# Moving GpSimd's division, the gather and the feed-forward layers by half a step in an attention kernel with routed rows

## The chip, the cores and the metric

The kernel runs on one core of one Trainium2 chip. A core has a matrix engine (TensorE, "PE" in the profile, with its weight loads as "PEld"), a vector engine (VectorE, "DVE"), an engine for activation functions and copies (ScalarE, "ACT"), a general engine (GpSimd, "POOL") and SyncE ("SP"), which here only issues DMAs. Each engine takes its own instructions in the order in which they were issued and waits on semaphores for the others. The metric is the time of one execution on the device in microseconds, the median of several runs.

## The reference

Two blocks in sequence: an attention with queries averaged in pairs, and a layer that passes only the 128 best-scored rows of each batch through a small network.

```python
B, H, S, D = 8, 8, 1152, 64            # attention; then rows of H * D = 512, F = 1024
q_pool = q.reshape(B, H, S // 2, 2, D).mean(axis=3)
attn = softmax(q_pool @ k.T / sqrt(D))
x = (attn @ v) -> (B, S // 2, H * D)   # heads side by side
scores = einsum('bsd,d->bs', x, w_gate)
out = x.copy()
for b in range(B):
    top_idx = argpartition(-scores[b], 128)[:128]
    xe = x[b, top_idx]
    ye = maximum(xe @ w1, 0) @ w2
    out[b, top_idx] = xe + sigmoid(scores[b, top_idx])[:, None] * ye
```

## The kernel before

All is float32. Two heads make a pair, four pairs a batch, 32 pairs in all. A pair's 576 averaged queries are split into two halves of 288, so that the main loop in `run` goes over 64 halves; half h has s = h % 2, and "even" and "odd" below mean s = 0 and s = 1. Each half is worked on over several turns of the loop (a turn is also called a half below, by the half whose scores it computes):

- turn h: `scores` (L818): 9 chunks of 4 matmuls with 64 rows each, keys down the partitions. ScalarE takes the exponential of each chunk (L825) into `p`. `folded` sums over the keys: GpSimd adds two thirds of the chunks (three instructions, L857, into `acc`), VectorE folds the last third and then `acc` (L862, two instructions) and reduces both to `sum` (L872).
- turn h + 1: `weighted` (L836): 36 matmuls that multiply `p` with the values. ScalarE copies the result out of PSUM (`two`, L844), GpSimd adds its two parts (`av`, L846), and `drained` transposes that on VectorE (`avb`, L915).
- turn h + 2: `multiplied`: GpSimd multiplies `avb` with the gate's weights (`prod`, L925).
- turn h + 3: `gated`: VectorE sums that (`red`, L979) and, with the pair's second half, divides it by the sums of exponentials (`part`, L981).

The sums of a pair come from 4 groups of partitions: ScalarE puts them side by side (`groups`, L887, in an even turn), VectorE adds them (`total`, L893), and ScalarE spreads the total over the partitions (`sums`, L902, in the odd turn). `normalized`, at the end of an odd turn, takes the reciprocal (`rec`, L954, VectorE) and multiplies `avb` by it on GpSimd (`x`, L956). `stored` sends `x` to the output (L968) two turns later. Even turns also prepare the next pair: GpSimd adds the queries (`qp`, L732), VectorE transposes keys and queries (`kT`, `qT`, L735 and L739). SyncE's queue has the loads of keys, queries and values, the stores and some small transfers of the routing, in the order of issue.

When a batch's last pair is gated, in turn h0 = 8b + 10, the generator `routed` begins for it. It does the row routing in pieces and stops at each `yield`. The mark that it yields says where it goes on: in `units(mid=True)`, called after the scores and before the weighted values of a turn, or in `units(mid=False)`, at the turn's end. Its pieces: sums of the gate's scores and their copy through DRAM (h0 + 1), counting ranks on VectorE (L1083, L1092, L1102; ends of h0 + 3, h0 + 4, h0 + 5), ranks and gates through DRAM to all partitions (`lines`, end of h0 + 5), two searches for slot i's row and gate (`pick`, L1166, end of h0 + 6), the row's number as an integer (`index`, L1175, GpSimd), the gather of the 128 rows from the output (L1183, an indirect DMA from GpSimd's queue), their transposes (L1197, TensorE, middle of h0 + 8), layer one (L1208, 32 matmuls, middle of h0 + 9), layer two (L1221, 8 matmuls, middle of h0 + 10), the scaling (`y`, L1240, ScalarE), the addition (L1245, GpSimd) and the scatter (L1246, an indirect DMA). A batch begins every 8 turns, so that the layers of one batch fall beside the first pieces of the next.

Batch 5 stops after layer one and batch 6 before its layers; both go on at the end, when the last batch is ranked: their matmuls fill TensorE's waits for it. The last batch's row of scores is made on TensorE (L1054) from `diag` (L1044), and its sums by a matmul (L938). `pieces(unit, n)` runs n pieces of a unit. The names at the end: `older`, `old` and `new` are batches 5, 6 and 7.

Of the kernel before, what the change touches and what calls it, by code (L numbers as in the profile page):

```python
# [10 lines left out]
P = 128  # L11
BLK = 32
# [522 lines left out]
class _Plain:  # L535
# [396 lines left out]
    def normalized(self, pair):  # L932

        nc, hp = self.nc, pair["hp"]
        tot = self.sums[:, pair["b"] * self.NPAIR + hp, :]
        if self.last_pair(pair):
            ps = self.banks()[:, 0, :]
            nc.tensor.matmul(  # L938
                ps[:, 0 : 2 * self.QB],
                lhsT=self.merge.rearrange("p g j -> p (g j)"),  # L940
                rhs=pair["sum"].rearrange("p j n -> p (j n)"),
                start=True,
                stop=True,
            )
            for j in range(2):
                rows = slice(j * self.D, (j + 1) * self.D)
                nc.scalar.activation(
                    tot[rows, :],
                    ps[rows, j * self.QB : (j + 1) * self.QB],
                    AF.Identity,  # L950
                    bias=self.tiny[rows, 0:1],
                )
        rec = pair["rec"] = self.small.tile([P, self.QB], F32, name="rec")
        nc.vector.reciprocal(rec[:, :], tot)  # L954
        x = self.work.tile([P, self.QB, BLK], F32, name="x")
        nc.gpsimd.tensor_tensor(  # L956
            out=x[:, :, :],
            in0=pair["avb"][:, :, :],
            in1=rec[:, :].unsqueeze(2).broadcast_to([P, self.QB, BLK]),
            op=ALU.mult,  # L960
        )
        pair["x"] = x

    def stored(self, pair):

# [7 lines left out]
    def gated(self, half):  # L973

        nc, pair, hb = self.nc, half["pair"], self.HB
        if half["s"] == 0:
            pair["red"] = self.small.tile([P, self.QB], F32, name="red")
        ns = slice(half["s"] * hb, (half["s"] + 1) * hb)
        nc.vector.tensor_reduce(pair["red"][:, ns], pair["prod"][:, ns, :], AX.X, ALU.add)  # L979
        if half["s"] == 1:  # L980
            nc.vector.tensor_tensor(  # L981
                out=pair["part"][:, pair["hp"], :],
                in0=pair["red"][:, :],
                in1=pair["rec"][:, :],
                op=ALU.mult,
            )
            if pair["hp"] == self.NPAIR - 1:
                unit = self.routed(pair["b"], pair["part"])
                at = next(unit) == "mid"
                self.routing.append([pair["b"], unit, at])  # L990

# [3 lines left out]
    def routed(self, b, part):  # L997
# [139 lines left out]
        for s0, w in self.slots:  # L1137
# [3 lines left out]
            if b == self.B - 1:  # L1141

                nc.vector.tensor_tensor(
                    out=pick[:, :, 0:w],
                    in0=self.slot_f[:, s0 : s0 + w].unsqueeze(1).broadcast_to([P, NT, w]),
                    in1=rank[:, :].unsqueeze(2).broadcast_to([P, NT, w]),
                    op=ALU.is_equal,
                )
                yield True
                ps = self.banks()[:, 0, 0:2]  # L1150
                for t, rows in tiles:
                    nc.tensor.matmul(
                        ps[0:w, :],
                        lhsT=pick[0:rows, t, 0:w],
                        rhs=meta[0:rows, t, :],
                        start=(t == 0),
                        stop=(t == NT - 1),
                    )
                nc.scalar.copy(index[0:w, :], ps[0:w, 0:1])
                nc.scalar.copy(own_gate[0:w, :], ps[0:w, 1:2])  # L1160
            else:
                yield True

                found = self.small.tile([P, 1], F32, name="found_token")
                for of, to in ((self.token_line, found), (lines[:, :, 1, :], own_gate)):
                    nc.vector.scalar_tensor_tensor(  # L1166
                        out=pick.rearrange("p t i -> p (t i)").rearrange("p (i t) -> p i t", t=NT)[0:w],
                        in0=lines[0:w, :, 0, :],
                        scalar=self.token[0:w, s0 // P : s0 // P + 1],
                        in1=of[0:w, :, :],  # L1170
                        op0=ALU.is_equal,
                        op1=ALU.mult,
                        accum_out=to[0:w, :],
                    )
                nc.gpsimd.tensor_scalar(  # L1175
                    out=index[0:w, :],
                    in0=found[0:w, :],
                    scalar1=float(b * Sp),
                    scalar2=None,
                    op0=ALU.add,  # L1180
                )
            xe = ffn.tile([P, self.Dm], F32, name="xe")
            nc.gpsimd.indirect_dma_start(  # L1183
                out=xe[0:w, :],
# [4 lines left out]
                oob_is_err=False,  # L1189
            )  # L1190
            yield True
            yield mid

            xeT = ffn.tile([P, self.ND, P], F32, name="xeT")
            pv = self.banks()[:, 0, :].rearrange("p (c n) -> p c n", n=P)
# [94 lines left out]
        )  # L1290
        return count_i

    def units(self, mid):


        for entry in self.routing[::-1]:
            b, unit, at = entry
            if b in self.waiting or at != mid:
                continue
            end = next((mark for mark in unit if mark), None)  # L1300
            if end is None:
                self.routing.remove(entry)
            elif end == "hidden" and b == self.B - 3:
                self.waiting.add(b)
            entry[2] = end in ("mid", "hidden") and b < self.B - 2

    def run(self):
        nc = self.nc
# [10 lines left out]
            self.load_values(loaded)  # L1319
        self.load_gate()  # L1320
        weights = self.weight_loads()
        for h in range(n_halves + 1):
            if h < n_halves:
                n, s = divmod(h, 2)
                if s == 0:
                    pair = upcoming
                    if pair["hp"] == 0:
                        part = self.ffn.tile([P, self.NPAIR, self.QB], F32, name="part")
                    pair["part"] = part
                else:  # L1330
                    loaded = None
                    if n + 2 < len(pairs):
                        loaded = self.load_pair(*pairs[n + 2])
                        self.load_values(loaded)
                    if n > 1:
                        self.stored(halves[h - 4]["pair"])
                if h > 1:
                    next(weights, None)
                half = {"pair": pair, "s": s}
                halves.append(half)  # L1340
                self.scores(half)
                if h > 1:

                    of = halves[h - 2 - s]["pair"]
                    if s == 0:
                        of["groups"] = self.side_by_side(of["sum"].rearrange("p j n -> p (j n)"))
                    else:
                        self.spread(of)
                self.units(mid=True)
                if h > 2:  # L1350
                    self.gated(halves[h - 3])
                self.folded(half)
                if h > 1:
                    self.multiplied(halves[h - 2])
                if s == 0 and loaded:
                    upcoming = loaded
                    self.prepare_pair(upcoming)
            else:
                self.stored(halves[h - 3]["pair"])
                self.gated(halves[h - 3])  # L1360
                self.multiplied(halves[h - 2])
                self.units(mid=True)
                self.units(mid=False)
            if h > 0:
                done = halves[h - 1]
                self.weighted(done)
                self.drained(done)
            if h == n_halves:
                self.multiplied(done)
                self.gated(halves[h - 2])  # L1370
            if 1 < h < n_halves and s == 0:
                done["pair"]["total"] = self.added(done["pair"]["groups"])
            if h == n_halves:
                self.normalized(done["pair"])
            elif h > 2 and s == 1:
                self.normalized(halves[h - 2]["pair"])
            if h < n_halves:
                self.units(mid=False)
        for _ in weights:
            pass  # L1380

        self.stored(halves[-1]["pair"])


        self.gated(halves[-1])
        left = [unit for _, unit, _ in self.routing]
        new = left.pop()
        old = left.pop() if left else iter(())
        older = left.pop() if left else iter(())
        assert not left  # L1390

        def pieces(unit, n=None):
            for i, _ in enumerate(unit):
                if i + 1 == n:
                    break

        pieces(older, self.NFC - 2)
        pieces(new, 1)
        pieces(older, 2)
        pieces(new, 3)  # L1400
# [71 lines left out]
```

## Time and profile before

| what | us |
|---|---|
| median of 3 runs (708.6 to 709.43) | 708.87 |
| the profiled execution | 706.64 |
| its span, first to last instruction | 704.8 |
| TensorE busy, 9948 matmul records | 694.4 |
| VectorE busy | 496.5 |
| GpSimd busy | 485.1 |
| ScalarE busy | 444.5 |

A line of a timeline gives the start in us from the beginning of the span, the duration, the engine, the line of the code, the operation, what it writes and reads, and how many instructions were merged (x72: each float32 matmul has two records). Square brackets hold the idle time of the engine before it and what ended it. Matmul ends are modelled, so that neighbouring groups overlap by some tenths: distances are taken from start to start. Among the groups of the page, with busy time, mean duration and idle time before them:

```profile
L857 POOL TENSOR_TENSOR acc<-p 128x576 f32<-128x576 f32 x192 | 266.3, 1417 | 15.4 <-ACT p L825 15.1
L846 POOL TENSOR_TENSOR av<-two 128x288 f32<-128x288 f32 x64 | 51.2, 800 | 96.5 <-ACT two L844 94.9
L956 POOL TENSOR_TENSOR x<-avb,rec 128x576 f32<-128x576 f32 x32 | 37.1, 1159 | 40.3 <-DVE rec L954 27.9
L732 POOL TENSOR_TENSOR qp<-qb 128x576 f32<-128x576 f32 x31 | 43.8, 1414 | 2.2 <-DMA qb<-in_q_dram 2.2
```

### The profile page before, as it was taken

How to read it: one execution, taken by the hardware profiler on the slowest of the kernel's cores; microseconds unless marked ns; L12 is line 12 of the kernel's file. 1: busy time of each engine (PE TensorE's matmuls, PEld its weight loads, DVE VectorE, ACT ScalarE, POOL GpSimd, SP SyncE). 2: the span in 40 equal slices, each digit the busy share in tenths (PEclk: the TensorE clock that was granted, in tenths of full speed). 3: DMA queues.
4: the chain of work that ended last, by engine and by line, in shares of the span. 5: the costliest groups of instructions: out<-in, count | busy, mean ns of one | idle time of the engine just before them, and what ended most of it. 6: DMA issues, size and time to landing. Idle time of an engine off the chain costs nothing.

```text
span 704.8 us, 23397 instructions
## 1 busy us (share of the span) xinstructions
PE 694.4 (99%) x9948; PEld 516.8 (73%) x9948; DVE 496.5 (70%) x793; ACT 444.5 (63%) x963; POOL 485.1 (69%) x452
## 2 busy tenths in 40 slices
PE   8999999999999999999999999999999999999996
PEld 5668899996758866688656887578775787766573
DVE  3877777996559965498754988559774697689540
ACT  6677778777547775477746776467754777477210
POOL 5877777868658695586955779467874877686520
PEclk9999999999999999999999999999999999999999
DMA  8888887858486483756928468382775728432200
GB/s 175 172 178 180 171 166 137 146 116 161 85 149 111 85 162 75 145 97 111 172 40 159 81 129 160 66 148 61 161 130 85 135 56 169 83 72 62 45 31 35
DMA packets 389490, 82.86 MB, mean 118 GB/s; under 512 B 376640, under 2 KB 376640, under 8 KB 389376
## 3 DMA queue, kind: packets, MB, share of 16 engines
q1 hardware_dynamic: 387872, 76.49, 58.1%
q0 software_dynamic: 1280, 4.20, 1.8%
q8 instruction: 80, 1.31, 0.8%
q10 hardware_dynamic: 224, 0.59, 0.3%
q14 instruction: 34, 0.28, 0.1%
HBM read 69.65 MB, written 11.59 MB: 115 GB/s over the span
## 4 chain that ended last, share of the span: by engine, by line
PE 89%; POOL 5%; issue 2%; DMA 1%; ACT 1%; DVE 1%; SPq 0%; POOLq 0%; DVEq 0%; ACTq 0%
PE ps L836 36%; PE ps L818 36%; PE ps L1208 8%; PE ps L1221 7%; POOL acc L857 2%; ACT p L825 1%; DMA kb<-in_k_dram 1%; DMA xe<-out_dram,index 1%; PE ps L1197 1%; POOL prod L925 1%; POOL x L956 0%; POOL av L846 0%; DVE fold L862 0%; POOL index L1175 0%; SPq L759 0%
## 5 line engine op out<-in xcount | busy, mean ns | idle before, releaser
L825 ACT ACTIVATE p<-ps 128x576 f32<-128x576 f32 x576 | 320.2, 695 | 1.7 <-PE ps L818 1.3
L818 PE MATMUL ps<-qT,kT 64*64 64x288 f32 x4608 | 295.2, 404 | 0.2 <-ACT p L825 0.2
L836 PE MATMUL ps<-p,v_sb 64*64 64x288 f32 x4608 | 294.6, 403 | 0.0
L857 POOL TENSOR_TENSOR acc<-p 128x576 f32<-128x576 f32 x192 | 266.3, 1417 | 15.4 <-ACT p L825 15.1
L836 PEld LDWEIGHTS ps<-p,v_sb 64*64 64x64 f32 x4608 | 215.5, 133 | 65.3 <-ACT p L825 9.2
L818 PEld LDWEIGHTS ps<-qT,kT 64*64 64x64 f32 x4608 | 208.0, 132 | 73.0 <-ACT p L825 15.4
L862 DVE TRANSPOSE_TENSOR_REDUCE fold<-p 128x54 f32<-128x1728 f32 x64 | 126.0, 1969 | 50.2 <-ACT p L825 50.2
L862 DVE TRANSPOSE_TENSOR_REDUCE fold<-acc 128x54 f32<-128x1728 f32 x64 | 125.3, 1957 | 46.0 <-POOL acc L857 45.8
L844 ACT COPY two<-ps 128x576 f32<-128x576 f32 x64 | 40.9, 639 | 156.9 <-PE ps L836 143.8
L846 POOL TENSOR_TENSOR av<-two 128x288 f32<-128x288 f32 x64 | 51.2, 800 | 96.5 <-ACT two L844 94.9
L915 DVE STREAM_TRANSPOSE avb<-av 128x288 f32<-128x288 f32 x64 | 29.4, 460 | 66.5 <-POOL av L846 66.5
L956 POOL TENSOR_TENSOR x<-avb,rec 128x576 f32<-128x576 f32 x32 | 37.1, 1159 | 40.3 <-DVE rec L954 27.9
L1208 PEld LDWEIGHTS ps<-xeT,w 128*128 128x128 f32 x512 | 57.8, 192 | 2.7 <-ACT p L825 2.6
L1208 PE MATMUL ps<-xeT,w 128*128 128x128 f32 x512 | 59.3, 277 | 0.0
L1221 PE MATMUL ps<-w,hT 128*128 128x512 f32 x128 | 57.3, 598 | 0.0
L925 POOL TENSOR_TENSOR prod<-avb,w_gate 128x288 f32<-128x288 f32 x64 | 51.5, 805 | 0.6 <-DVE avb L915 0.6
L902 ACT ACTIVATE sums<-total,tiny 32x18 f32<-32x18 f32 x124 | 38.1, 308 | 15.9 <-DVE total L893 14.2
L732 POOL TENSOR_TENSOR qp<-qb 128x576 f32<-128x576 f32 x31 | 43.8, 1414 | 2.2 <-DMA qb<-in_q_dram 2.2
L1221 PEld LDWEIGHTS ps<-w,hT 128*128 128x128 f32 x128 | 23.6, 190 | 28.1 <-issue 25.8
L735 DVE STREAM_TRANSPOSE kT<-kb 128x1152 f32<-128x1152 f32 x31 | 42.5, 1370 | 0.0
L887 ACT COPY groups<-sum 32x36 f32<-32x36 f32 x124 | 27.1, 219 | 6.7 <-DVE sum L872 5.2
L981 DVE TENSOR_TENSOR part<-red,rec 128x18 f32<-128x18 f32 x32 | 27.0, 845 | 1.1
(95 smaller groups left out, 290.6 us busy)
## 6 DMA issues: line engine op xcount, KB each, us to landing
kb<-in_k_dram SPq DMA_DIRECT2D x124, 144.0 KB
qb<-in_q_dram SPq DMA_DIRECT2D x124, 144.0 KB
v_sb<-in_v_dram SPq DMA_DIRECT2D x124, 144.0 KB
out_dram<-x SPq DMA_DIRECT2D x128, 72.0 KB
lines<-row_rank SPq DMA_DIRECT2D x7, 640.0 KB
w<-in_moe_w_dram SPq DMA_DIRECT2D x8, 512.0 KB
sc_row<-row SPq DMA_DIRECT2D x7, 288.0 KB
acc<-in_q_dram ACTq DMA_DIRECT2D x2, 288.0 KB
```

Source lines behind the costliest of these rows:

```text
L732: nc.gpsimd.tensor_tensor(out=qp[:, :, :], in0=pair["q"][:, :, 0, :], in1=pair["q"][:, :, 1, :], op=ALU.add)
L735: nc.vector.transpose(kT.rearrange("p (c g i) -> p c g i", c=self.NC, i=BLK), pair["k"].rearrange("p (g c) d -> p c g d", c=self.NC),)
L818: nc.tensor.matmul(sc[keys, j, 0:n], lhsT=pair["kT"][rows, c * P + keys.start : c * P + keys.stop], rhs=pair["qT"][rows, qs], start=True, ...
L825: nc.scalar.activation(p[:, c // G, c % G, :, :], sc[:, :, 0:n], AF.Exp, scale=self.scale)
L836: nc.tensor.matmul(av[j * self.D : (j + 1) * self.D, e, 0:n], lhsT=half["pair"]["v"][keys, j, c, :], rhs=half["p"][keys, c // G, c % G, j, :],
L844: nc.scalar.copy(two[:, :, :], av[:, :, 0:n])
L846: nc.gpsimd.tensor_tensor(out=half["av"][:, :], in0=two[:, 0, :], in1=two[:, 1, :], op=ALU.add)
L857: nc.gpsimd.tensor_tensor(out=acc[:, u, :], in0=units[:, 0, u, :], in1=units[:, 1, u, :], op=ALU.add)
L862: nc.vector.tensor_reduce(fold[:, a, :], of.rearrange("p u (m d) -> p (u m) d", d=BLK), AX.X, ALU.add, apply_transpose=True,)
L925: self.nc.gpsimd.tensor_tensor(out=pair["prod"][:, ns, :], in0=pair["avb"][:, ns, :], in1=self.w_gate[:, hp : hp + 1, :].broadcast_to([P, ...
L1208: nc.tensor.matmul(pv[:, f, 0:w], lhsT=self.w1[:, c, (f0 + f) * P : (f0 + f + 1) * P], rhs=xeT[:, c, 0:w], start=(c == 0), stop=(c == self ...
L1221: nc.tensor.matmul(ps[0:w, 0 : self.Dm], lhsT=hT[:, f, 0:w], rhs=self.w2[:, f, :], start=(f == 0), stop=(f == self.NFC - 1),)
```

## The change

Five edits. `normalized` keeps the reciprocal, and the multiplication to `x` becomes `divided`, called at the end of the following even turn. The `index` is computed by VectorE, directly behind the picks, and the gather goes out in a new place, `units("sums")`, between GpSimd's sums and its `prod` of the next turn (for batch 6 at that turn's end). Transposes and both layers of batches 0 to 5 come one turn later. `added` (the totals) stands ahead of `prepare_pair`. The loop's extra last turn is taken out of the loop and written in another order: weighted values of the last two halves one behind the other, batch 6's transposes behind six layer-two matmuls of batch 5, and both remaining `x` behind both remaining `prod`.

```diff
-        rec = pair["rec"] = self.small.tile([P, self.QB], F32, name="rec")
-        nc.vector.reciprocal(rec[:, :], tot)
-        x = self.work.tile([P, self.QB, BLK], F32, name="x")
-        nc.gpsimd.tensor_tensor(
+        pair["rec"] = self.small.tile([P, self.QB], F32, name="rec")
+        nc.vector.reciprocal(pair["rec"][:, :], tot)
+
+    def divided(self, pair):
+
+        x = pair["x"] = self.work.tile([P, self.QB, BLK], F32, name="x")
+        self.nc.gpsimd.tensor_tensor(
             out=x[:, :, :],
             in0=pair["avb"][:, :, :],
-            in1=rec[:, :].unsqueeze(2).broadcast_to([P, self.QB, BLK]),
+            in1=pair["rec"][:, :].unsqueeze(2).broadcast_to([P, self.QB, BLK]),
             op=ALU.mult,
         )
-        pair["x"] = x
...
-                nc.gpsimd.tensor_scalar(
+                nc.vector.tensor_scalar(
                     out=index[0:w, :],
                     in0=found[0:w, :],
...
+
+                yield "sums"
             xe = ffn.tile([P, self.Dm], F32, name="xe")
             nc.gpsimd.indirect_dma_start(
...
             yield True
-            yield mid
+            if b < self.B - 2:
+                yield True
+            if b != self.B - 2:
+                yield mid
...
-    def units(self, mid):
+    def units(self, at):
...
-            if b in self.waiting or at != mid:
+            if b in self.waiting or place != at:
                 continue
...
-            entry[2] = end in ("mid", "hidden") and b < self.B - 2
+            entry[2] = self.place(b, end)
+
+    def place(self, b, mark):
+        if mark in (True, None) or b >= self.B - 2:
+            return "end"
+        return "mid" if mark == "hidden" else mark
...
+            self.units("mid")
+            if h > 2:
                 self.gated(halves[h - 3])
+            self.folded(half)
+            self.units("sums")
+            if h > 1:
                 self.multiplied(halves[h - 2])
-                self.units(mid=True)
-                self.units(mid=False)
+            if h > 1 and s == 0:
+                last = halves[h - 1]["pair"]
+                last["total"] = self.added(last["groups"])
+            if s == 0 and loaded:
+                upcoming = loaded
+                self.prepare_pair(upcoming)
             if h > 0:
-                done = halves[h - 1]
-                self.weighted(done)
-                self.drained(done)
-            if h == n_halves:
-                self.multiplied(done)
-                self.gated(halves[h - 2])
-            if 1 < h < n_halves and s == 0:
-                done["pair"]["total"] = self.added(done["pair"]["groups"])
-            if h == n_halves:
-                self.normalized(done["pair"])
-            elif h > 2 and s == 1:
+                self.weighted(halves[h - 1])
+                self.drained(halves[h - 1])
+            if h > 2 and s == 1:
                 self.normalized(halves[h - 2]["pair"])
-            if h < n_halves:
-                self.units(mid=False)
+            if h > 3 and s == 0:
+
+                self.divided(halves[h - 3]["pair"])
+            self.units("end")
...
-        self.stored(halves[-1]["pair"])
-
-
-        self.gated(halves[-1])
-        left = [unit for _, unit, _ in self.routing]
-        new = left.pop()
...
-        pieces(older, self.NFC - 2)
+        self.gated(halves[-3])
+        self.weighted(halves[-1])
+        self.drained(halves[-1])
+        self.multiplied(halves[-2])
+        self.multiplied(halves[-1])
+        self.gated(halves[-2])
+        pieces(older, 1)
+        self.normalized(halves[-1]["pair"])
+        for half in (halves[-3], halves[-1]):
+            self.divided(half["pair"])
+            self.stored(half["pair"])
+        self.gated(halves[-1])
+        _, new, _ = self.routing.pop()
+
+        pieces(older, self.NFC - 3)
+        pieces(old, 1)
         pieces(new, 1)
```

## The prediction

> **What bounds the kernel now.** I read the busy table first, then the chain that ended last, then TensorE's own timeline from start to end, and last the timeline of all engines around each place where TensorE lost time.
>
> ```profile
> span 704.8 us, 23397 instructions
> PE 694.4 (99%) x9948; PEld 516.8 (73%) x9948; DVE 496.5 (70%) x793; ACT 444.5 (63%) x963; POOL 485.1 (69%) x452
> PE 89%; POOL 5%; issue 2%; DMA 1%; ACT 1%; DVE 1%; SPq 0%; POOLq 0%; DVEq 0%; ACTq 0%
> ```
>
> TensorE is busy for 99% of the span and the chain runs through it for 89%. No other engine is near: the most that a rearrangement can win is TensorE's lost time. So I took that time stage by stage, as the distance from the start of one group of TensorE's timeline to the start of the next. A stage of 36 score or 36 weighted-value matmuls (the trace has each as two records, so x72) takes 4.37 us nearly everywhere, and 4.48 when a 128-row matmul follows it (171.64 to 176.12, 514.65 to 519.12; 4.53 behind one). Between 8.7 and 643 us six stages are clearly longer, all of them the scores (L818) that stand before the transposes of a batch's chosen rows (L1197). Three of them:
>
> ```profile
> 247.48 4.81 PE L818 MATMUL ps<-qT,kT 64*64 64x288 f32 x72
> 252.22 0.66 PE L1197 MATMUL ps<-ident,xe 128*128 128x128 f32 x4
> ...
> 424.04 0.63 PE L1197 MATMUL ps<-ident,xe 128*128 128x128 f32 x4
> ...
> 590.49 4.91 PE L818 MATMUL ps<-qT,kT 64*64 64x288 f32 x72
> 595.71 0.63 PE L1197 MATMUL ps<-ident,xe 128*128 128x128 f32 x4 [0.31 <-ACT p L825]
> ```
>
> Start to start the six last 4.68, 4.74, 4.81, 5.33 (418.71 to 424.04), 4.80 and 5.22 us: over 4.48 that is 0.20 + 0.26 + 0.33 + 0.85 + 0.32 + 0.74 = 2.70 us. What happens there, in the timeline of all engines:
>
> ```profile
> 246.71 1.14 POOL L1183 DMA_INDIRECT xe<-out_dram,index  x1 [0.28 <-POOL index L1175]
> 248.16 0.64 ACT L844 COPY two<-ps 128x576 f32<-128x576 f32 x1 [2.22 <-PE ps L836]
> ...
> 248.84 0.15 PEld L818 LDWEIGHTS ps<-qT,kT 64*64 64x64 f32 x4 [0.16 <-ACT two L844]
> ...
> 417.82 0.92 POOL L1175 TENSOR_SCALAR index<-found_token 128x1 int32<-128x1 f32 x1 [2.95 <-DVE pick L1166]
> 419.02 1.14 POOL L1183 DMA_INDIRECT xe<-out_dram,index  x1 [0.28 <-POOL index L1175]
> ...
> 419.02 4.89 DMA xe<-out_dram,index
> ```
>
> The copy of the weighted values (L844) normally starts 0.33 us after the next scores do (581.76, then 582.09). Here it starts 0.68 after (247.48, then 248.16), and TensorE's weight load waits for it, because the copy frees a bank of PSUM. In five of the six places GpSimd is issuing the gather at that moment. In the sixth (418.71) the copy is on time, and instead the two exponentials after it, which fall inside the gather's issue, are each held some 0.3 us for TensorE. So ScalarE hears of TensorE about 0.3 us late while that gather is being issued. The last line is another loss: in that batch the rows land 4.89 us after issue, at 423.9, just when the transposes start.
>
> At the end TensorE loses time twice more:
>
> ```profile
> 648.00 4.59 PE L836 MATMUL ps<-p,v_sb 64*64 64x288 f32 x72
> 653.20 0.63 PE L1197 MATMUL ps<-ident,xe 128*128 128x128 f32 x4 [0.61 <-DMA xe<-out_dram,index]
> 653.76 4.59 PE L836 MATMUL ps<-p,v_sb 64*64 64x288 f32 x72
> 658.29 0.41 PE L938 MATMUL ps<-sum,merge 128*128 128x36 f32 x2
> 658.53 5.40 PE L1221 MATMUL ps<-w,hT 128*128 128x512 f32 x12
> 664.28 0.97 PE L1054 MATMUL ps<-diag,ones 128*128 128x288 f32 x3 [0.35 <-DVE rank_parts L1076]
> ```
>
> Batch 6's gather is waited for at 653.20, and the last batch's row of scores (L1054) at 664.28. From 664.28 on TensorE runs nearly without a gap to the end.
>
> [...] the record lasts 1.06 to 1.27 us, the landing is 2.8 to 5.8 us after issue. [...] (L1102 takes 0.27 to 1.57 us)[...].
>
> **The change part by part.**
>
> *x a half later (L956 moves from `normalized` to `divided`).* Nothing is added: 32 multiplies of 1159 ns. Where it stood, GpSimd waited for VectorE's reciprocal: 27.9 us in 17 waits, up to 3.2. Behind it were the three sums of exponentials (L857), and behind those VectorE's second fold (0.85 us waits at 239.70 and 412.01). Now the reciprocal is a half old. GpSimd's even halves hold 3 x 1.38 + prod 0.79 + qp 1.41 + av 0.79 + x 1.16 = 8.29 us, the odd ones 5.72; a half is 8.74, so it fits. The stores (L968) are issued in the same half as before: SyncE reaches them some 12 us into it, behind the loads (165.93 with the half's scores at 153.23), and x is due about 3 us into it, so no queue is held. Worth nothing by itself.
>
> *Index on VectorE, gather behind the next half's sums.* Seven GpSimd instructions of 920 ns and the 2.96 us wait in front of each go; VectorE gets seven small ones. Before shows none; the similar L1283 takes 0.14 us, the read of an accumulator 0.08: I take 0.15, between 0.08 and 1.3 (a lockout such as L1102 shows), so 1 us of VectorE in all and none of the span unless VectorE is late. When is the gather issued now? VectorE's second pick ends 7.6 us after the start of scores of the half that follows (246.35 - 238.75); the fold wait of 0.85 and the gate wait of 0.27 (both for GpSimd) should go and the index be added: 6.6 us. GpSimd's sums of that half can start when the fourth exponential is done, 0.87 + 0.14 + 4 x 0.556 = 3.2 us in, and end at 7.4. So the gather runs from about 7.4 to 8.6. The copy it disturbed is due at 8.74 + 0.33 = 9.07. The disturbance before ended 0.1 to 0.4 us after the gather's record, so up to 9.0: it just clears. That margin is the weakest number here.
>
> *Transposes and layers a half later.* TensorE does the same 4 + 32 + 8 matmuls per batch. The rows get 8.7 us more to land, so the waits for the DMA at 424 and 595 go. Layer two (7.06 us) then stands in the half where the ranking begins on VectorE, still between scores and weighted values. The scatter moves to an odd half, where GpSimd has room: 5.72 + 0.24 + 1.28 + 1.04 = 8.28 us.
> From these two parts I expect 2.70 back, less 0.15 that I leave for one or two places: **2.55 us**, bounds 0.9 (only the landing waits of the two worst places go, about 0.5 and 0.4) and 2.7.
>
> *Totals in front of the transposes.* L893 (0.35 us) goes ahead of kT, qT and avb (1.37 + 0.74 + 0.45). ScalarE's sums (L902) waited 14.2 us for it, in 7 waits, but no stage of TensorE is longer behind one. kT is 0.35 us later, with 3.5 us to spare (its partner qT ends at 244.00, its scores start at 247.48). Nothing either way.
>
> *Last half reordered.* In before, the stretch 648.00 to 664.28 is 16.28 us. Its work: weighted 4.37 + 4.48, L938 0.24, six layer-two matmuls at 7.03 / 8 = 0.88 each, 5.27, transposes 0.44 (as at 680.68): 14.80. The transposes of batch 6 now come after five of those six, so one switch between 64-row and 128-row matmuls goes too. Will the inputs be there? With T the end of the last weighted stage, TensorE reaches L1054 at T + 6.0. The copy ends at T + 0.97 (0.33 + 0.64); av then starts at once instead of behind x and prod, ends T + 1.8; avb 2.3; prod 3.4 (the other prod lies in front of it); red 3.9; part 4.5; line 4.8; diag T + 5.6. 0.4 us to spare. Batch 6's gather goes out behind the av of the half before, 2.6 us before T (0.97 + 0.79 into the last stage of 4.37), lands by T + 3.2 (5.8 us at most) and is needed at T + 5.5. The two x go behind both prods, their stores end some 12 us after T, and the last gather comes 18 us after it. So 1.48, of which I take **1.35**; bounds 0.6 (L1054 still waits) and 1.5.
>
> Sum: 2.55 + 1.35 = 3.9 us. The profiled execution has a span of 704.8 and took 706.64, so 700.9 and 702.7. The median of the three runs shown is 708.87, 2.2 above that execution; the same 3.9 off it gives **705.0**.
>
> **Rivals.** (a) The gather still hits the copy, because GpSimd's sums end later than 7.4 us or the lateness isn't tied to the gather at all: in these stages the DMA engines are 0.89 to 1.06 busy (0.74 in the undisturbed one from 204.01), and the loads stay where they are. For the gather speaks that the held instruction changes with its position at 418.71. Then 0.9 + 1.35 = 2.25 us are won: 706.6. (b) The last half isn't gained because diag is late, though the copies are on time: 2.55 + 0.3, 706.0 to 706.3; the margin of 0.4 us is small, but av no longer stands behind x. (c) What is won is lost at new places and the time stays within 0.2% (1.4 us, about what a measurement of this kernel can tell from no change): 708.5. TensorE's 4.37 us everywhere else speaks against it. (d) Slower, by a VectorE backlog. From the ranking's start to the pick VectorE has hardly a gap (215.2 to 239), and the change gives it the index and puts x beside its two-input operations[...]. qT of that half ends 13.98 us after the half's scores start (244.00 - 230.02) and is needed at 17.46: 3.5 us of slack, 2.4 in the batch at 401.25. A backlog beyond that stops TensorE itself, once per batch. From 3.5 + 3.9 / 6 = 4.1 us on it eats the gain; at 4.5 to 5 it costs 6 to 9 us, 711 to 714. Against it: what is added is 0.15 us, and about 1.1 us of waits go.
>
> **How the numbers follow.** Forecast (704.0 to 706.0): 0.60. (a) and (b) together (706.0 to 707.4): 0.16. (c): 0.10. (d): 0.14. The range leaves out (d), half of (c) and a little below: 703.8 to 708.5. Faster by over 0.2%: 0.76; within: 0.10; slower: 0.14.
>
> **What would show it.** Right: scores stages before the transposes at 4.48 us, L844 starting 0.33 us after the next scores in the halves with a gather, no wait of x for the reciprocal, the gather issued 7.4 us into its half, and 14.8 us from the start of the last-but-one weighted stage to L1055. Wrong: those stages still at 4.7 to 4.8 (then the gather wasn't the cause or wasn't moved clear), a wait at L1055, or stages of scores that wait for qT.

## The result, and the profile after

The changed kernel takes 728.23 us (median of 6 runs, 727.28 to 731.47) against 708.74 for the kernel before on the same chip: ratio 1.0285, 95% interval 1.026 to 1.0311. It is 2.85% slower, where 705.0 us was predicted. Here and below a ratio is taken against runs of the kernel before in the same session (medians 706.87 to 708.74 us); it is not the quotient of the two medians.

The page of the kernel after, its span, busy table and chain:

```profile
span 726.6 us, 23365 instructions
PE 700.5 (96%) x9948; PEld 511.9 (70%) x9948; DVE 541.4 (75%) x800; ACT 448.0 (62%) x963; POOL 480.4 (66%) x445
PE 67%; DVE 16%; issue 4%; POOL 4%; ACT 3%; DMA 3%; SPq 3%; POOLq 0%; DVEq 0%; ACTq 0%
```

The span of the profiled execution grew by 21.8 us. VectorE is 45 us busier with seven instructions more, and its share of the chain went from 1% to 16%. Its groups say which instructions grew (busy, mean ns, then idle before), first in before, then in after:

```profile
L981 DVE TENSOR_TENSOR part<-red,rec 128x18 f32<-128x18 f32 x32 | 27.0, 845 | 1.1
L1102 DVE SCALAR_TENSOR_TENSOR tie<-sc_row,gate_sc,before 128x128 f32<-128x128 f32 (+1 forms) x40 | 24.0, 600 | 0.0
```

```profile
L983 DVE TENSOR_TENSOR part<-red,rec 128x18 f32<-128x18 f32 x32 | 50.9, 1590 | 1.1
L1103 DVE SCALAR_TENSOR_TENSOR tie<-sc_row,gate_sc,before 128x128 f32<-128x128 f32 (+1 forms) x40 | 44.5, 1113 | 0.0
L959 POOL TENSOR_TENSOR x<-avb,rec 128x576 f32<-128x576 f32 x32 | 36.9, 1156 | 0.0
```

`part` took 845 ns on average before and takes 1590 now; `tie`, which counts equal scores in the ranking, 600 and 1113. The last line is the other side: `x` waited 40.3 us on GpSimd before, and now not at all, as intended. A mean of 1590 hides the shape: the `part` instructions last from 0.18 to 9.86 us. VectorE's timeline around the first of three long ones:

```profile
341.66 0.39 DVE L981 TENSOR_REDUCE red<-prod 128x9 f32<-128x288 f32 x1
342.09 9.86 DVE L983 TENSOR_TENSOR part<-red,rec 128x18 f32<-128x18 f32 x1
351.98 0.27 DVE L1008 TENSOR_REDUCE line<-part 128x18 f32<-128x72 f32 x1
...
357.88 0.72 DVE L739 STREAM_TRANSPOSE qT<-qp 128x576 f32<-128x576 f32 x1
```

and GpSimd's at the same time:

```profile
337.00 1.13 POOL L1186 DMA_INDIRECT xe<-out_dram,index  x1 [3.20 <-DVE index L1176]
338.17 0.81 POOL L925 TENSOR_TENSOR prod<-avb,w_gate 128x288 f32<-128x288 f32 x1
338.93 0.80 POOL L846 TENSOR_TENSOR av<-two 128x288 f32<-128x288 f32 x1
339.69 4.13 POOL L857 TENSOR_TENSOR acc<-p 128x576 f32<-128x576 f32 x3
...
346.67 1.15 POOL L959 TENSOR_TENSOR x<-avb,rec 128x576 f32<-128x576 f32 x1
347.79 4.12 POOL L857 TENSOR_TENSOR acc<-p 128x576 f32<-128x576 f32 x3
359.04 0.80 POOL L925 TENSOR_TENSOR prod<-avb,w_gate 128x288 f32<-128x288 f32 x1 [7.13 <-DVE avb L915]
```

A product of 128 x 18 elements that takes 0.18 us elsewhere starts at 342.09 and ends at 351.95. In all that time GpSimd runs without a gap: the wait of 3.20 us for the index left it behind, and it catches up with everything ready. It first pauses at 351.91, and there the product ends. The trace shows no wait here but one instruction that has started and doesn't finish, so that no table of waits names it. TensorE's timeline shows what hangs on it, and the table by stretches how TensorE then runs (busy us of five engines, granted clock, DMA share, GB/s; the last row is an undisturbed scores stage):

```profile
348.94 4.59 PE L836 MATMUL ps<-p,v_sb 64*64 64x288 f32 x72
358.75 6.69 PE L818 MATMUL ps<-qT,kT 64*64 64x288 f32 x72 [5.21 <-DVE qT L739]
365.37 7.41 PE L1214 MATMUL ps<-xeT,w 128*128 128x128 f32 x64
```

```profile
core 0: us, PE busy (x) PEld busy (x) DVE busy (x) ACT busy (x) POOL busy (x), PEclk, DMA share, GB/s
348.94:358.75 9.81, 4.60 (x74) 2.69 (x73) 9.74 (x9) 2.71 (x11) 2.97 (x3) 0.87 0.94 170
358.75:361.00 2.25, 2.25 (x20) 1.39 (x24) 2.25 (x3) 1.75 (x5) 1.63 (x3) 0.50 0.44 75
361.00:363.20 2.20, 2.20 (x24) 1.23 (x20) 2.17 (x3) 1.58 (x3) 0.00 (x0) 0.54 0.00 0
363.20:365.37 2.17, 2.17 (x41) 1.13 (x33) 1.92 (x6) 2.17 (x5) 1.66 (x2) 1.00 0.01 1
267.77:272.25 4.48, 4.48 (x77) 2.60 (x69) 3.07 (x7) 4.18 (x8) 2.05 (x3) 1.00 0.88 190
```

VectorE's queue behind `part` holds `qT`, and TensorE waits 5.21 us for it. Then the next scores take 6.62 us in place of 4.48, because for over 4 us the granted clock is 0.50 to 0.54. So one held product costs TensorE twice. The same pair of stages, start to start, at the three places: 9.81 + 6.62, 9.78 + 6.16 and 9.79 + 5.91 us. Less the usual 4.53 + 4.48 this is 7.4 + 6.9 + 6.7 = **21.0 us**.

The gains that were predicted for single stages are there in this same execution: the scores stages ahead of the transposes take 4.48 to 4.55 us (before 4.68 to 5.33; 2.4 us less over the six), and the last stretch is 15.06 us (670.43 to 685.49; before 16.28). What uses them up, so that the growth of 21.8 us looks like the three places alone, is mainly the start: the scores at 23.93 stood at 22.23 in before, and the mean clock up to there is 0.93 in place of 1.00. No edit touches the start, and it varies between the executions shown below (22.1 to 23.9). The rest is small: after the start no other stage is over 0.6 us longer.

### The profile page after: what moved, and what is told of

Its sections match the earlier page's. It is cut to its first block, busy times and chain, and to the rows that moved or that the text cites. A ratio compares the mean times of both kernels' runs of the same rounds, so it can differ in the third digit from the quotient of the medians.

```text
span 726.6 us, 23365 instructions
## 1 busy us (share of the span) xinstructions
PE 700.5 (96%) x9948; PEld 511.9 (70%) x9948; DVE 541.4 (75%) x800; ACT 448.0 (62%) x963; POOL 480.4 (66%) x445
## 3 DMA queue, kind: packets, MB, share of 16 engines
q8 instruction: 80, 1.31, 0.8%
## 4 chain that ended last, share of the span: by engine, by line
PE 67%; DVE 16%; issue 4%; POOL 4%; ACT 3%; DMA 3%; SPq 3%; POOLq 0%; DVEq 0%; ACTq 0%
PE ps L818 27%; PE ps L836 26%; PE ps L1214 8%; PE ps L1227 5%; DVE fold L862 5%; DVE part L983 4%; ACT p L825 3%; POOL acc L857 2%; DVE tie L1103 2%; DVE kT L735 1%; SPq L710 1%; SPq L707 1%; DMA qb<-in_q_dram 1%; DMA kb<-in_k_dram 1%; DVE qT L739 1%
## 5 line engine op out<-in xcount | busy, mean ns | idle before, releaser
L818 PE MATMUL ps<-qT,kT 64*64 64x288 f32 x4608 | 299.6, 409 | 15.6 <-DVE qT L739 15.6
L836 PEld LDWEIGHTS ps<-p,v_sb 64*64 64x64 f32 x4608 | 210.4, 133 | 70.6 <-ACT p L825 9.9
L862 DVE TRANSPOSE_TENSOR_REDUCE fold<-p 128x54 f32<-128x1728 f32 x64 | 126.0, 1970 | 58.8 <-ACT p L825 58.8
L862 DVE TRANSPOSE_TENSOR_REDUCE fold<-acc 128x54 f32<-128x1728 f32 x64 | 123.8, 1934 | 0.4 <-POOL acc L857 0.4
L983 DVE TENSOR_TENSOR part<-red,rec 128x18 f32<-128x18 f32 x32 | 50.9, 1590 | 1.1
L1103 DVE SCALAR_TENSOR_TENSOR tie<-sc_row,gate_sc,before 128x128 f32<-128x128 f32 (+1 forms) x40 | 44.5, 1113 | 0.0
```

Of the source, the lines that this page charges most:

```text
L818: nc.tensor.matmul(sc[keys, j, 0:n], lhsT=pair["kT"][rows, c * P + keys.start : c * P + keys.stop], rhs=pair["qT"][rows, qs], start=True, ...
L836: nc.tensor.matmul(av[j * self.D : (j + 1) * self.D, e, 0:n], lhsT=half["pair"]["v"][keys, j, c, :], rhs=half["p"][keys, c // G, c % G, j, :],
L862: nc.vector.tensor_reduce(fold[:, a, :], of.rearrange("p u (m d) -> p (u m) d", d=BLK), AX.X, ALU.add, apply_transpose=True,)
L983: nc.vector.tensor_tensor(out=pair["part"][:, pair["hp"], :], in0=pair["red"][:, :], in1=pair["rec"][:, :], op=ALU.mult,)
L1103: nc.vector.scalar_tensor_tensor(out=tie[0:rows, 0:rows], in0=sc_row[0:rows, at : at + rows], scalar=own, in1=self.before[0:rows, 0:rows], ...
```

## The experiments

The question after this: is `x` in its new place the cause, or the index for which GpSimd now waits with everything else behind it? And is it really the second input of `part` that is held?

**x put back, everything else as in after; and x moved alone.**

```diff
# e1: after, with
-            if h > 3 and s == 0:
-                self.divided(halves[h - 3]["pair"])
+                self.divided(halves[h - 2]["pair"])      # in "if h > 2 and s == 1"
# e2: before, with
+            elif h > 3 and s == 0:
+                self.divided(halves[h - 3]["pair"])      # and no x in normalized
```

> The changed kernel with x (L956/L959) put back to the end of the odd turn, where GpSimd waits for the reciprocal; everything else of the change stays. Theory 1 (x later is the cause: without its wait GpSimd's two-input instructions follow one another unbroken and VectorE's two-input part is held until the run ends): no part over 2 us, no wait of scores for qT, 704 to 707 us. Theory 2 (the gather's wait for the index in its new place is the cause: it makes GpSimd late, and it then catches up in an unbroken run): three parts of near 10 us stay, 722 to 730 us.

> The kernel before with x alone moved to the end of the even turn. Theory 1: parts of several us appear and the kernel is slower than before, 714 to 730 us. Theory 2: parts stay under 2 us, 706 to 710 us.

With `x` back: 706.52 us, ratio 0.9985 (0.9977 to 0.9992). Moved alone: 721.62 us, ratio 1.0189 (1.0172 to 1.0206). So moving `x` is enough to lose, and putting it back is enough to lose nothing; the index and the gather's place aren't the cause of the loss. First with `x` back (the groups), then with `x` alone (VectorE's timeline):

```profile
L959 POOL TENSOR_TENSOR x<-avb,rec 128x576 f32<-128x576 f32 x32 | 37.0, 1157 | 58.8 <-DVE rec L954 43.2 <-DVE total L893 7.7 <-DVE rank_parts L1075 5.9
L983 DVE TENSOR_TENSOR part<-red,rec 128x18 f32<-128x18 f32 x32 | 23.5, 735 | 1.1
```

```profile
346.34 0.40 DVE L981 TENSOR_REDUCE red<-prod 128x9 f32<-128x288 f32 x1
346.77 10.43 DVE L983 TENSOR_TENSOR part<-red,rec 128x18 f32<-128x18 f32 x1
...
362.84 0.74 DVE L739 STREAM_TRANSPOSE qT<-qp 128x576 f32<-128x576 f32 x1
```

With `x` back GpSimd waits 58.8 us in front of it (40.3 in before), and no `part` lasts over 0.93 us. But little is won either: the scores stages ahead of the transposes take 4.48 to 4.53 us, and five stages of weighted values have become longer, four 4.83 to 4.85 us and one 5.89 (TensorE waits there for VectorE, 1.31 us for `line`). With `x` moved alone GpSimd waits 1.5 us, and `part` at six places lasts 10.42, 10.45, 10.43, 10.44, 10.43 and 6.31 us. So the wait of `x` for the reciprocal, which the prediction counted as a loss to be removed, kept VectorE's two-input product short. In before the first `part` starts at 42.52, 0.27 us after `x`, and ends at 43.44, where `x` does (43.41), although GpSimd goes on to its sums without a gap: it was let in at the first boundary.

**part without a second input; and a pause for part.** The first replaces the product by a reduction that reads `red` alone, and so leaves the division by the sum of exponentials out of the gate's scores. The second adds one small GpSimd instruction behind every pair's product, so that GpSimd waits until `part` is written.

```diff
# e3: after, with
-            nc.vector.tensor_tensor(out=part, in0=red, in1=rec, op=ALU.mult)
+            nc.vector.tensor_reduce(part, red.unsqueeze(2), AX.X, ALU.add)
# e4: after, with, behind the product
+            nc.gpsimd.tensor_scalar(out=seen, in0=part[:, 0:1], scalar1=-88.0, op0=ALU.max)
```

> The changed kernel, with part made by a reduction over one element that reads red alone: the division by the row's sum is left out of the gate's scores. If VectorE is held because the instruction has two inputs in SBUF (theories 1 and 2 alike): part takes 0.2 us everywhere, no wait for qT, 703 to 707 us. If VectorE is held for another reason (a semaphore, its queue): the 10 us stay before or in another instruction, 722 to 730 us.

> The changed kernel, with one small GpSimd instruction behind each part that reads one column of it, so that GpSimd can't start the next sums before VectorE's part has ended (about 0.25 us of GpSimd per pair, and its wait). If an unbroken run of GpSimd holds part: part under 1.5 us, no wait for qT, 703 to 707 us, and below the kernel before. If part is slow for another reason: GpSimd waits for the 10 us as well, 722 to 735 us.

One input: 703.64 us, ratio 0.9942 (0.9925 to 0.9958). With the pause: 703.83 us, ratio 0.995 (0.9933 to 0.9967). The groups of the first, then of the second:

```profile
L1100 DVE SCALAR_TENSOR_TENSOR tie<-sc_row,gate_sc,before 128x128 f32<-128x128 f32 (+1 forms) x40 | 44.9, 1122 | 0.0
L983 DVE TENSOR_REDUCE part<-red 128x18 f32<-128x18 f32 x32 | 5.5, 172 | 1.1
```

```profile
L990 POOL TENSOR_SCALAR seen<-part 128x1 f32<-128x1 f32 x32 | 7.3, 229 | 71.0 <-DVE part L983 68.8 <-ACT p L825 2.2
L983 DVE TENSOR_TENSOR part<-red,rec 128x18 f32<-128x18 f32 x32 | 6.1, 192 | 1.1
```

The reduction is never held (172 ns), although it stands at the same place beside the same GpSimd work; so what is held is the product with its two inputs (a product with one input was not run). The `tie` is as slow as in after (1122 ns) and costs nothing: the whole loss was `part`. And with the pause GpSimd idles 68.8 us for `part`, and nothing is lost by it: the scores stages ahead of the transposes take 4.53 to 4.55 us, the weighted values behind them 4.41 or 4.42. This kernel beats both others. The gain over before is 4.0 us by the medians, 3.5 by the ratio: about what the prediction had expected of the change.

**The hold by itself.** A program without the reference's work, run once: VectorE multiplies 128 x 18 elements (two inputs in SBUF) beside k GpSimd additions of 128 x 576 in a row; each case three times.

> The reference's work is left out: a bare program in which GpSimd runs k additions of two 128x576 tiles one behind the other, and VectorE starts one 128x18 instruction that hangs on nothing but a small GpSimd instruction ahead of them. k = 1, 3, 6, 12 with a VectorE multiplication of two SBUF inputs; k = 6 with a 128x1 GpSimd memset in the middle; k = 6 with a VectorE reduction of one input; three of each. If VectorE's instruction waits for one GpSimd instruction at most: 1 to 2 us for every k. If it waits for the end of an unbroken run: 1.3, 4, 8 and 16 us for k = 1, 3, 6, 12, some 4 us with the memset if that lets it in, and 0.2 us for the reduction.

| beside | VectorE's instruction, us |
|---|---|
| 1 addition | 1.35, 1.35, 1.35 |
| 3 | 1.35, 1.35, 1.35 |
| 6 | 1.35, 8.12, 1.35 |
| 12 | 1.36, 16.24, 1.35 |
| 6, a 128 x 1 memset in the middle | 1.35, 4.06, 8.15 |
| 6, VectorE reduces instead (one input) | 0.17, 0.17, 0.17 |

VectorE's and GpSimd's timeline at the longest:

```profile
62.11 16.24 DVE L1335 TENSOR_TENSOR held<-go,small_e 128x18 f32<-128x18 f32 x1 [15.10 <-POOL go L1325]
```

```profile
62.04 16.28 POOL L1332 TENSOR_TENSOR sum<-src_a,src_b 128x576 f32<-128x576 f32 x12
```

In the plain cases there are two outcomes and nothing between: let in at the first boundary between two GpSimd instructions (1.35 us), or held to the end of the unbroken run. There are only two holds among them, one beside 6 additions and one beside 12. A memset in between let it in once and once not. Neither of the two theories had this.

The kernel after has it too. In five batches `part` meets the same GpSimd instructions in the same order, none with a gap: in three it is held 9.84 to 9.86 us, in two it gets in at the second boundary and lasts 1.75 and 1.76. With `x` moved alone all six were held. What decides isn't known. And in the kernel a hold can end inside an unbroken run: in five batches of after a `tie` of 4.52 to 4.54 us gets in where GpSimd goes on from its sums to `prod` without a gap. VectorE's timeline, then GpSimd's:

```profile
218.90 4.54 DVE L1103 SCALAR_TENSOR_TENSOR tie<-sc_row,gate_sc,before 128x128 f32<-128x128 f32 x1
```

```profile
219.15 4.13 POOL L857 TENSOR_TENSOR acc<-p 128x576 f32<-128x576 f32 x3
223.24 0.85 POOL L925 TENSOR_TENSOR prod<-avb,w_gate 128x288 f32<-128x288 f32 x1
224.06 1.39 POOL L732 TENSOR_TENSOR qp<-qb 128x576 f32<-128x576 f32 x1
```

**Where did the lateness beside the gather come from?** Before, with the gather issued twice in a row, and before with only the last half reordered.

```diff
# e6: before, behind the gather
+            nc.gpsimd.indirect_dma_start(...)            # the same rows again, into pick
# e7: before, with after's last half (weighted values of the last two halves together,
#     batch 6's transposes behind six layer-two matmuls); x stays in normalized
```

> The kernel before with the gather of batches 0 to 7 issued twice in a row, the second time into a tile that nobody reads. If the gather's issue makes ScalarE hear of TensorE late: the stages of scores ahead of the transposes grow from 4.7 to 4.8 us to over 5.0, and the kernel is 2 us or more slower, 709.5 to 713. If the lateness there comes from the load on the DMA engines: they grow by under 0.1 us, 707 to 709.

> The kernel before with nothing but the last half reordered as in the change (its x stays where it was). By the prediction's sum 1.35 us fewer than before: the stretch from the last-but-one weighted stage to L1054 goes from 16.3 to 14.8 to 15.1 us, 706.0 to 707.2 us where before is 707.8. If the order at the end gives nothing: 707.5 to 708.2.

The gather twice: 707.57 us, ratio 1.001 (0.9994 to 1.0027). Its timelines of GpSimd, then of ScalarE:

```profile
246.71 1.12 POOL L1183 DMA_INDIRECT xe<-out_dram,index  x1 [0.28 <-POOL index L1175]
248.14 1.01 POOL L1191 DMA_INDIRECT pick<-out_dram,index  x1 [0.30 <-issue]
```

```profile
247.83 0.64 ACT L844 COPY two<-ps 128x576 f32<-128x576 f32 x1 [1.90 <-PE ps L836]
```

The gather starts at the very moment it had before, and the copy is on time: 0.35 us after the scores at 247.48, and 0.35 to 0.37 in all six places. The stages ahead of the transposes are 4.57, 4.55, 4.55, 4.55, 4.55 and 4.96 us. So the gather's issue isn't what delays ScalarE; the excess of these stages changes from execution to execution of the same loop (in the second of these kernels 4.57, 4.55, 5.19, 4.64, 4.56 and 5.21). What caused it stays open.

The last half alone: 706.28 us, ratio 1.0007 (0.999 to 1.0023): no difference that can be measured. Its trace has 15.67 us in the last stretch, 0.6 less than before; there TensorE waits 0.71 us at the row of scores for `diag`, which ends at 662.80 where the transposes are done at 662.2: late, as rival (b) had it, though `diag` itself takes 0.76 us as in before.

**x behind diag, on top of the pause.** In after and with the pause, `diag` takes 1.35 us in place of 0.76, because the two last `x` run beside it.

```diff
# e8: the kernel with the pause (left out for the last pair), with
+            nc.gpsimd.tensor_scalar(out=seen, in0=diag[:, 0, 0:1], ...)
+        self.gated(halves[-1])                           # ahead of the two x
         for half in (halves[-3], halves[-1]):
             self.divided(half["pair"])
             self.stored(half["pair"])
-        self.gated(halves[-1])
```

> e4_wait_part with the two last x held back behind VectorE's diag, which took 1.35 us beside x where it took 0.76 in the kernel before. If diag is held by x: diag 0.8 us, no wait of TensorE at its matmul, 0.2 to 0.3 us less than e4_wait_part, 703.0 to 703.8. If not: diag stays at 1.3 us, 703.5 to 704.5.

704.16 us, ratio 0.9958 (0.9945 to 0.9971): not to be told from the pause alone. `diag` is back at 0.76 us, and TensorE's timeline does show it:

```profile
645.73 8.96 PE L836 MATMUL ps<-p,v_sb 64*64 64x288 f32 x144
...
660.53 1.14 PE L1068 MATMUL ps<-diag,ones 128*128 128x288 f32 x4
```

14.80 us, to the hundredth what the prediction's sum of the work gave; the median can't resolve the last 0.26.

**Is the pause free? The same pause in before's order, with x later and without.**

```diff
# e9: the kernel with only x moved, and e10: before; in both, behind the product
+            nc.gpsimd.tensor_scalar(out=seen, in0=part[:, 0:1], scalar1=-88.0, op0=ALU.max)
```

> Before with only x moved (721.62 us earlier), and one small GpSimd instruction behind every gated second half that reads one column of part, so that GpSimd must pause until VectorE has written it. Theory 1, x later is slow only because its wait for the reciprocal was the pause in which VectorE got its two-input product in: the 14 us vanish, 706 to 708 us, ratio to before 0.997 to 1.001, part at 0.2 to 1.4 us everywhere, no weighted-value stage over 5 us for qT. Theory 2, x in its new place is in itself too late or crowds GpSimd's even halves: the time stays over 715 us.

> Before itself with the same small GpSimd instruction that reads part. Theory 1, before already has its pause (GpSimd's wait for the reciprocal), so a second one buys nothing: ratio 0.998 to 1.002, with part's mean falling from 0.85 to about 0.2 us and no stage of TensorE shorter for it. Theory 2, the wait is worth something of its own and the 4 us that after with this wait gains over before come from it and not from the moved gather, transposes and last half: ratio 0.993 to 0.997.

737.19 us (ratio 1.0402, 1.037 to 1.0434) and 736.29 us (1.0394, 1.0353 to 1.0434): both theories of the second run are wrong, and of the first only the number of theory 2 (over 715 us) came about, not its reason, since before's own place of `x` is as slow. `part` is no longer held (215 ns on average with `x` later), and the time is worse than ever. Before with the pause, GpSimd's timeline, then TensorE's:

```profile
616.70 0.92 POOL L1183 TENSOR_SCALAR index<-found_token 128x1 int32<-128x1 f32 x1 [2.97 <-DVE pick L1174]
617.90 1.13 POOL L1191 DMA_INDIRECT xe<-out_dram,index  x1 [0.28 <-POOL index L1183]
```

```profile
615.36 1.72 PE L818 MATMUL ps<-qT,kT 64*64 64x288 f32 x24
617.83 3.44 PE L818 MATMUL ps<-qT,kT 64*64 64x288 f32 x48 [0.76 <-ACT two L844]
623.88 0.63 PE L1205 MATMUL ps<-ident,xe 128*128 128x128 f32 x4 [2.60 <-DMA xe<-out_dram,index]
```

In before the gather went out 0.76 us ahead of the scores that precede the transposes (589.73 against 590.49); with the pause it goes out 2.5 us behind them. GpSimd, which waits for VectorE, and VectorE, whose fold waits for GpSimd (79.3 us over the kernel, 45.8 in before), have both become some 3 us later. The rows land too late, and the copy too, because ScalarE's `sums` in front of it wait for the total (35.3 us over the kernel, 14.2 in before). The six stages take 7.84 to 8.84 us, 20.6 us more than the same six in before's profile.

**The pause in after's order, but the rows' work a half earlier.** What does after's order have that before's lacks?

```diff
# e11: the kernel with the pause, with
-            if b < self.B - 2:
-                yield True                               # transposes and layers one turn later
```

> After with the wait for part (703.83 us), with transposes and layers of batches 0 to 5 put back one half earlier; the gather stays where after has it, between the sums and the product. Theory 1, the half that the change gives the rows is what pays for GpSimd's pause: in that run the gather goes out 3.9 us after its half's scores start and rows land up to 5.8 us after issue, while the transposes would stand 4.5 us after that start, so each of batches 0 to 5 stalls TensorE 4 to 6 us in front of its transposes (for the DMA), and some of them cost 1 to 2 us more by the lower clock after it: 726 to 745 us, ratio to before 1.025 to 1.055. Theory 2, the later rows are no cover for the pause, and the 30 us of the two runs with before's order came from the index on GpSimd and the totals behind the transposes alone: 703 to 708 us, no wait for the gather over 1 us.

746.52 us, ratio 1.053 (1.0496 to 1.0565): theory 1, at the upper end of its ratios and just above its 745 us. The stages ahead of the transposes take 8.25 to 9.11 us, with waits of 3.6 to 4.5 us just in front of these, and the weighted values after them 6.10 to 7.01. The kernel with the pause, which differs by that one line, has no such wait. So the half that the change gives the rows is worth far more here than a late copy. The same line without the pause was not run. In after the gather goes out 1.92 us into the half in question (337.00, scores at 335.08), and its rows land 5.1 us after issue. That is some 2.5 us after the scores' 4.48: an estimate from this trace, by which after's order needs that half without the pause as well.

## Why the prediction was wrong

- **"x a half later … Worth nothing by itself."** This is the step that failed. It was priced as work: 32 multiplies that fit into GpSimd's even halves, and 27.9 us of waits gone. They do fit, and the waits are gone, but the waits were needed: beside a GpSimd that doesn't pause `part` can be held to the end of GpSimd's run, three times 9.8 us here. x alone cost 1.89%.
- **The bound of the lockout, 1.3 us.** The prediction took it from rows of before like `tie` (0.27 to 1.57 us). Those were instructions let in at the next boundary (the `tie` of 1.57 us starts at 398.58 and ends at 400.15, where one of GpSimd's sums ends, 400.01); the other outcome, a hold over a whole run (9.86 us), did not occur in before's trace (no `part` over 0.92 us, no `tie` over 1.57), so no row of before bounded it. It was used for `index` alone, and for `part` no hold was counted at all. In the runs the product with two inputs was held and the reduction in its place (0.17 us) was not, and a hold reached over up to 12 GpSimd instructions (16.24 us).
- **Rival (d), "VectorE backlog"**, had 0.14 of the chance. That end came about, at the place it named (`qT`), but from a held instruction and not from added work, in three batches and not in all six, and at 728 us, not 711 to 714. That it is the right place is in part luck. Its argument against itself, that "about 1.1 us of waits go", was true of VectorE's waits (those of the second fold for GpSimd fell from 45.8 to 0.4 us over the kernel) but weighed nothing against a hold of 9.86. Its price counted a wait of TensorE as that wait alone; 2.1, 1.7 and 1.4 us came on top from the clock.
- **The index**, taken at 0.15 us, took 0.14 to 0.15. But "the gather runs from about 7.4 to 8.6" failed: at 337.00 it is 10.65 us into the half that began at 326.35, as GpSimd waits 3.20 us for the index. The copy was already done by then.
- **The gather's 2.55 us.** The size was read off one execution. The stages are at 4.48 to 4.55 us in after and with the pause, as predicted; but the reading "ScalarE hears of TensorE about 0.3 us late while that gather is being issued" is refuted by the doubled gather: where these stages did become shorter, it was not for the reason given.
- **The last half, 1.35 us**: 1.22 in after and with the pause, 1.48 with `x` behind `diag`. The "0.4 us to spare" of `diag` was missed by its longer time beside `x` (1.35 us in place of 0.76). Alone, this part made no difference that could be measured.
- **Totals in front: "Nothing either way."** Not tested alone. In before with the pause ScalarE's `sums`, in front of the copy, wait for the total, and TensorE up to 0.83 us for that copy. Whether an earlier total would help there was not run.

The sum of 3.9 us fits another kernel, the change with GpSimd pausing for `part` (703.83 us, 4.0 below before). That is luck in part: the larger of its two terms was read off one execution and given a cause that the runs refute.

## What to carry to other kernels

Before removing an engine's wait, look for who works beside it: with GpSimd's wait ahead of `x`, VectorE's product of two inputs in SBUF lasted at most 0.93 us here, without it up to 10.45, so the idle time of an engine that is not the bottleneck may be what keeps another engine's instruction short. Such an instruction ahead of something critical should have one input (the reduction took 0.17 us), or GpSimd should be made to wait for it (`part` took 0.19 us on average, the kernel 703.83), but only where what GpSimd does next (here the gather) has the room: in before's order the same pause cost 3.94%. And read the longest record of a group, not its mean, and more than one execution where the loss is some tenths.

## What was unexpected of the hardware

- Beside a plain run of GpSimd additions, VectorE's two-input product either got in at the first boundary or was held to the run's end: 1.35 us or 8.12 beside 6 additions, 1.36 or 16.24 beside 12. In the kernel holds also ended at a boundary inside a run (`tie`, 4.54 us). What decides isn't known from these runs.
- A wait of TensorE of about 5 us cost 1.4 to 2.1 us more: in the next stage the granted clock was about half for 4.3, 3.4 and 2.8 us at the three places (an estimate from the mean clocks of stretches of 2.0 to 2.25 us, with a mean between 0.50 and 1.00 taken as a mixture of these two) and then 1.00. In before with the pause waits of 2.37 and 2.90 us were followed by weighted values of 6.05 and 6.10 us at a mean clock of 0.72, one of 2.50 by 5.52, others of 1.90, 2.43 and 2.60 by 4.41, 4.42 and 4.53. So the length of the wait alone doesn't tell which stage is slowed; what decides isn't known from these runs.
